# Infini-attention block on one core: stack loads moved eight slots later, maxima issued two slots sooner, and three small moves around the feed-forward part

## The chip, the core and the metric

The kernel runs on one core of a Trainium2 chip. The metric is the device time of one execution in microseconds (us); runs before and after are compared by the median of several. Five engines work side by side, each taking its own instructions in order: TensorE (PE in the profile; its weight loads PEld), VectorE (DVE), ScalarE (ACT), GpSimd (POOL) and SyncE (SP), which here only issues DMAs. ACT issues some DMAs as well.

## The reference, cut to what matters

A transformer block: adaptive layer norm, attention with a compressive memory (32 heads of 16, 4 segments of 512 rows), output projection, residual, a second layer norm, a feed-forward part of width 1792, residual.

```python
mod = (_silu(c) @ w_mod).reshape(c.shape[0], 6, 1, -1)
sa, ca, ga, sb, cb, gb = (mod[:, 0], mod[:, 1], mod[:, 2], mod[:, 3], mod[:, 4], mod[:, 5])
h = _layernorm(x, axis=-1) * (1 + ca) + sa
x = x + ga * _A_ref(h, A_wq, A_wk, A_wv, A_wo, A_beta)
h = _layernorm(x, axis=-1) * (1 + cb) + sb
x = x + gb * _B_ref(h, B_w1, B_b1, B_w2, B_b2)
...
# _A_ref, for each segment s of 512 rows (all heads):
logits = jnp.einsum("bhqd,bhkd->bhqk", qs, ks) * scale + mask
p = _softmax(logits, axis=-1)
a_dot = jnp.einsum("bhqk,bhkd->bhqd", p, vs)
num = jnp.einsum("bhld,bhde->bhle", pq, M)
den = jnp.einsum("bhld,bhd->bhl", pq, z)[..., None] + 1e-6
o = g * (num / den) + (1.0 - g) * a_dot
M = M + jnp.einsum("bhld,bhle->bhde", pk, vs)
z = z + jnp.einsum("bhld->bhd", pk)
```

x is 2048 x 512 in float32; products are formed from high and low halves, which gives three matmuls where one would do in plain precision.

## The kernel before

Up to about 180 us the conditioning, the projections and the memory parts run. From 180 to 470 us runs the attention, in loops. From 470 us the feed-forward part (FFN) runs, in products that combine sums of blocks (t1 to t4, b11 to b22).

**Stacks and loops.** The heads and segments are cut into 32 stacks Q of four heads, each with two pairs P = 2Q and 2Q + 1. A stack's keys and queries lie in two SBUF tiles, `kst` and `qst`, with four buffers each (Q modulo 4). `load_stacks(Q)` (L172 to L175) fetches rows 0 to 95 of both from DRAM with two DMAs of 384 KB on SP, kst first. One pass of the loop over Q (L1013) does, for the pairs of stack Q, the T parts (`st_part`, scores with queries along the free axis, PE L693, exp on ACT L708 and L719, causal cut on POOL L696) and the products with V (L733), and for the pairs of stack Q + 2 the S parts (`s_part`, PE L606 and L643 to L645, row maxima on DVE L613 and L617). S1 of stack Q + 2 is the first thing in loop Q: its weight loads and matmuls wait for the two loads of stack Q + 2. The order inside a loop is written out:

```python
ORDER = ('S1 c0 T2 T3 T2 c1 S2 c2 S3 T3 S3 c3 c4 c5 T5 S0 c6 c7 T0 c8 c9 '
         'T1 T4 S2 c10 c11 T5 S1 c12 T4 S0 c13 T0 c14 T1 c15 c16 c17 c18 c19')
```

S and T with a number are parts of `s_part` and `st_part`. c0 to c19 are twenty slots; a slot runs whatever has been put down for it. The table `PRM` (L27 to L75) gives places as slot numbers: a number d for stack Q means slot 20Q + d, counted from the start of loop 0, so -65 is c15 of loop Q - 4 and -57 is c3 of loop Q - 3. Each engine gets its instructions in the order in which the loop issues them.

**The maxima's way.** The row maxima of a stack (`nm`) are needed by its T parts as three further rows of `qst` (96 to 98). `m_rows` (POOL L661, two subtractions, slot -26) splits them into three bf16 parts; `m_put` (L664 to L669, slot -17) turns them with a matmul against the identity into a PSUM bank (PE L667, tile `pv`) and copies that on ACT (L127, tile `ms`, 48 x 128); `m_send` (L675) follows one slot later and writes 12 KB into the query stack by DMA, issued by SP for stacks 0 to 12 and by ACT for stacks 13 to 31 (`msa` 13). The first reader is the first T2 of loop Q. There is one `pv` bank, which the V products of each loop and `m_put` share; the copy `ts` (ACT L127) empties it at a loop's start, and its store to DRAM is `TD` on SP (L751). `dn` (L756) and `opk` (L758) bring pairs of those back in every second loop; the rows of L784, L788, L913 on SP are other small or 256 KB transfers.

**Other places.** `gate` is the slot of a 256 KB load of a gate vector on SP (L989). `ht` is the slots in which the four transposed blocks of segment 0 are made for the FFN (`ln2_turn`, PE L574, ACT L576). `r_sub` (DVE L886) forms the sums t1 to t4, `r_hi` copies the high half on ACT (L127) and `r_lo` subtracts it on DVE (L899). `rest` runs leftovers of the last stacks' attention (den L775, rb_in, mix L793, o_lo L810). `quad(n)` is the FFN's first half for quarter n in numbered steps; `bg` puts work into a step, here the transposes of segments 2 and 3.

Of the kernel before, what the change touches and what calls it, by code (L numbers as in the profile page):

```python
# [28 lines left out]
 'pv': [[31, 0, 0, 512], [36, 1, 128, 512], [37, 2, 256, 512], [38, 3, 384, 512]],  # L29
 'pvlast': [[25, 0, 0, 512], [30, 1, 128, 512], [31, 3, 384, 512], [35, 2, 256, 512]],  # L30
 'mrows': -26,
 'mput': -17,
 'stacks': -65,
 'den': 95,
 'dnl': 18,
 'rbl': 13,
# [11 lines left out]
 'wox': -25,  # L48
 'mixu': 12,
 'olou': 12,  # L50
 'ht': [502, 509, 516, 523],
 'ht1': 644,
 'ln': [{'in': [327, 367, 387, 407], 'stat': [418, 425, 437, 445], 'rstd': 449, 'on': [455, 475, 479, 495]},
        {'in': [527, 530, 547, 567], 'stat': [565, 577, 585, 597], 'rstd': 603, 'on': [624, 626, 628, 630]}],
 'wl': [26, 66, 77, 81],
 'gate': 197,
# [45 lines left out]
def block_kernel(ctx: ExitStack, tc: tile.TileContext, x, wq, wk, wv, wo, betaq, betam,  # L102
# [99 lines left out]
    with ExitStack() as pa:  # L202
# [124 lines left out]
        for ds in ((0,), (1, 2, 3)):  # L327
# [4 lines left out]
            n = slice(ds[0], ds[-1] + 1)  # L332
# [24 lines left out]
        rest = ((2, 3), (4, 5))  # L357
# [155 lines left out]
        for s in range(NSEG):  # L513
            for tok in PRM["A"][s].split():
                n = int(tok[1]) if len(tok) > 1 and tok[1].isdigit() else 0
# [64 lines left out]
    mm = psw.tile([128, 512], F32, name="mm")  # L580
# [3 lines left out]
    with ExitStack() as pb:  # L584
# [295 lines left out]
        def raw(p, n):  # L880
            return T2 if n == "t2" and p == 0 else hk(p, RAW.get(n, n))

        def r_sub(p, n, e=v):
            x, y = {"t1": ("b12", "b11"), "t2": ("b22", "t1"), "t3": ("b22", "b12"), "t4": ("b21", "t2")}[n]
            for o, i, j in zip(raw(p, n), raw(p, x), raw(p, y)):
                e.tensor_tensor(out=o, in0=i, in1=j, op=ALU.subtract)  # L886
# [6 lines left out]
        def r_hi(p, n, e=None):  # L893
            for k in range(2):
                copy(e or "a", R[n][0][k], raw(p, n)[k])
# [117 lines left out]
        for Q in range(-LEAD // 2, NP // 2 + 1):  # L1013
# [4 lines left out]
            for tok in ORDER.split():  # L1018
                n = int(tok[1:])
# [15 lines left out]
    def rest(U, *names):  # L1035
        for n in names:
            for x in [x for x in left if x[0] == n and x[1] == U]:
                left.remove(x)
                x[2]()

    with ExitStack() as pc:
# [6 lines left out]
        spare = pf.tile([128, 512], F32, name="spare")  # L1048
# [10 lines left out]
        def w_views(j, i):  # L1059
            t, lo, hi, src, o = WS[i]  # L1060
            x = (wb if src else wa)[j][:, o:o + hi - lo]
            return [z.rearrange("p a k n -> p (a k n)") for z in (wt1[t][j % 2][0][:, lo:hi], wt1[t][j % 2][1][:, lo:hi], x)]
# [5 lines left out]
        def w_lo(j, i):  # L1068
            h, l, x = w_views(j, i)
            v.tensor_tensor(out=l, in0=x, in1=h.bitcast(F32), op=ALU.subtract)  # L1070
# [24 lines left out]
        def bg(n, i, f, *a):  # L1095
            bgs.setdefault((n + i // 7, i % 7), []).append((f, a))
# [73 lines left out]
        r_lo(0, "t1")  # L1170
        r_hi(0, "t2")
        w_lo(0, 1)
        rest(15, "den", "rb_in")
        rest(14, "mem_mix")
        r_lo(0, "t2")
# [26 lines left out]
        for n in range(2 * FH):  # L1202
# [6 lines left out]
            if j + 1 < FH and n:  # L1209
                for i in range(7):  # L1210
                    bg(n, i, w_prep, n + 1, i)
        for n, i, f, *a in ((0, 0, rest, 14, "o_hi", "o_lo"), (0, 0, r_sub, 0, "t3"), (0, 0, r_sub, 0, "t4"), (0, 1, w_hi, 0, 2), (0, 1, w_hi, 0, 3),
                            (0, 3, r_hi, 0, "t3"), (0, 3, wo_late, 2, 3), (0, 3, r_lo, 0, "t3"), (0, 3, w_hi, 1, 0),
                            (0, 4, w_lo, 1, 0), (0, 4, w_lo, 0, 2), (0, 4, w_lo, 0, 3), (0, 4, load_w1, 2),
                            (0, 4, r_hi, 0, "t4"), (0, 4, rest, 15, "mix", "o_hi"), (0, 4, r_lo, 0, "t4"),
                            (0, 4, rest, 15, "o_lo"), (0, 5, g_out, 0, s1, s1, 0, 0), (0, 6, w_hi, 1, 1),
                            (2, 2, ln2_load, 2, 0), (2, 3, ln2_load, 2, 1), (2, 5, ln2_load, 2, 2), (2, 6, ln2_load, 2, 3),
                            (1, 0, w_lo, 1, 1), (1, 0, r_hi, 0, "b22"), (1, 1, wo_late, 3, 4),
                            (1, 1, w_hi, 1, 2), (1, 1, w_hi, 1, 3), (1, 1, r_lo, 0, "b22"), (1, 2, close_wo),
                            (1, 3, w_lo, 1, 2), (1, 3, w_lo, 1, 3)):  # L1220
            bg(n, i, f, *a)
# [14 lines left out]
        for s, n in ((2, 3), (3, 4)):  # L1236
            for b in range(4):
                bg(n, 1 + b, ln2_stats, s, b)
            bg(n, 5, ln2_rstd, s)
            for i in range(2):  # L1240
                bg(n, 8 + i, ln2_applies, s, 2 * i, 2 * i + 2)
            for d in range(KB):
                bg(n, 14 + d, ln2_turn, s, d, (mm, spare)[d % 2])

        w2r = {}

# [50 lines left out]
        for p in range(2):  # L1297
            n = FH * p + FH - 1
# [56 lines left out]
        for p in range(2):  # L1355
            for j in range(FH):
                quad(FH * p + j, j == 0)
            n = FH * p + FH - 1
# [3 lines left out]
            for m in range(NM):  # L1362
                s, f = 2 * p + m // FB, m % FB
# [68 lines left out]
```

## Time and profile before

| what | value |
|---|---|
| median of 3 runs | 785.66 us (785.25 to 789.05) |
| the profiled execution: time | 784.93 us |
| the profiled execution: span, first to last instruction | 783.2 us |
| PE busy | 764.9 us, 98% of the span |
| DVE, ACT, POOL busy | 555.9, 472.4, 316.3 us |
| granted TensorE clock | 1.000 |
| DMA moved | 156.09 MB, mean 199 GB/s |

The profile is of one execution, and 1.73 us lie outside its span. Rows of the timeline give the start in us, the length in us, the engine, the line, the operation with output<-input, and how many like instructions follow each other (x2); a bracket gives the idle time of the engine just before and what ended it. SPq and ACTq are DMA issues on the queues of SP and ACT. A row in the waits list is the waiting engine and line, the engine or DMA that released it, the sum of waits in us, how many, and the longest.

### The profile page before, as it was taken

To read this page: it belongs to the slowest core of one execution; us is meant where nothing else is said; L and a number is where in the kernel's file an instruction comes from. 1 tells how busy PE (TensorE), PEld (TensorE's weight loads), DVE (VectorE), ACT (ScalarE), POOL (GpSimd) and SP (SyncE) were. 2 spreads that over 40 slices of the span, in tenths; PEclk is the share of its full clock that TensorE was granted. 3 is DMA by queue.
4 is the path that set the end of the run, shared out by engine and by line. 5 is a ranking of instruction groups with operands and counts; after the bars stand their busy time and mean duration, and the time that the engine had idled before them with its cause. 6 is when DMAs were issued, how large, how long until landed. Compare 5 with 4: busy or idle time off the path is not lost.

```text
span 783.2 us, 14171 instructions
## 1 busy us (share of the span) xinstructions
PE 764.9 (98%) x4549; PEld 529.0 (68%) x4549; DVE 555.9 (71%) x1540; ACT 472.4 (60%) x910; POOL 316.3 (40%) x535
## 2 busy tenths in 40 slices
PE   9999999999999999999989999999999999999998
PEld 4877786877444445454445457787888888888887
DVE  6677677548989888888977898868569764432424
ACT  3465546364888877777768676766644446652221
POOL 1256458261468556665786671242000404200000
PEclk9999999999999999999999999999999999999999
DMA  9596956487465576768677755595666524545543
GB/s 337 185 295 228 317 179 221 166 275 258 139 187 166 175 207 190 212 205 243 185 188 210 222 156 166 184 309 177 202 240 208 184 95 162 172 148 166 173 126 116
DMA packets 108818, 156.09 MB, mean 199 GB/s; under 512 B 16324, under 2 KB 55620, under 8 KB 108744
## 3 DMA queue, kind: packets, MB, share of 16 engines
q1 hardware_dynamic: 106911, 153.39, 62.1%
q10 hardware_dynamic: 1833, 1.81, 0.7%
q8 instruction: 35, 0.57, 0.3%
q14 instruction: 39, 0.32, 0.1%
HBM read 93.95 MB, written 60.83 MB: 198 GB/s over the span
## 4 chain that ended last, share of the span: by engine, by line
PE 76%; DVE 8%; POOL 5%; DMA 4%; issue 4%; ACT 3%; ACTq 0%; SPq 0%; DVEq 0%; POOLq 0%
PE bx L1080 9%; PE att L693 6%; PE pv L733 6%; PE q L313 6%; PE bx L1349 6%; PE att L606 5%; PE by L1349 5%; PE bv L1349 5%; PE bv L1080 5%; PE k L313 4%; PE v L464 3%; PE mm L821 3%; DMA qst<-ms 3%; PE spare L1349 2%; PE by L1080 2%
## 5 line engine op out<-in xcount | busy, mean ns | idle before, releaser
L613 DVE CUSTOM_DVE_ANT_0 dump<-att,maskb 128x384 bf16<-128x384 f32 (+1 forms) x456 | 207.7, 512 | 36.2 <-PE att L606 17.9
L708 ACT ACTIVATE pt<-att 128x384 f32<-128x384 f32 (+1 forms) x256 | 125.6, 545 | 17.7 <-PE att L693 14.1
L696 POOL TENSOR_SCALAR_AFFINE_SELECT pt<-pt 128x256 f32<-128x256 f32 x256 | 105.5, 425 | 67.9 <-ACT pt L708 42.4
L693 PE MATMUL att<-qst,kst 99*128 99x256 bf16 (+3 forms) x512 | 107.7, 300 | 7.3 <-DMA qst<-ms 5.4
L606 PE MATMUL att<-kst,qst 96*128 96x384 bf16 (+1 forms) x456 | 103.9, 310 | 1.1 <-ACT pt L719 0.4
L693 PEld LDWEIGHTS <-kst 99*128 99x128 bf16 x512 | 43.8, 97 | 74.9 <-issue 37.7
L865 POOL TENSOR_TENSOR wb<-wa 128x256 f32<-128x256 f32 x24 | 20.1, 838 | 154.2 <-DMA wa<-in_w 123.1
L733 PE MATMUL pv<-pt,V 128*32 128x512 f32 (+1 forms) x992 | 79.8, 439 | 0.0
L719 ACT ACTIVATE pt<-att 128x256 f32<-128x256 f32 (+1 forms) x128 | 62.2, 494 | 27.8 <-PE att L693 15.4
L136 DVE TENSOR_TENSOR gl<-s,gh 128x512 fp32r<-128x512 f32 x34 | 24.1, 710 | 42.0 <-ACT gh L133 42.0
L606 PEld LDWEIGHTS <-qst 96*128 96x128 bf16 x456 | 37.9, 98 | 21.6 <-issue 14.2
L733 PEld LDWEIGHTS pv<-pt,V 128*32 128x32 f32 x992 | 25.8, 109 | 36.0 <-issue 30.4
L133 ACT ACTIVATE gh<-s 128x512 fp32r<-128x512 f32 x34 | 21.3, 628 | 46.8 <-PE spare L1349 18.7
L1085 ACT ACTIVATE s<-s,b1t 128x512 f32<-128x512 f32 x42 | 30.3, 722 | 21.3 <-DVE s L1089 21.1
L1089 DVE TENSOR_TENSOR s<-bv,s 128x512 f32<-128x512 f32 x28 | 19.2, 687 | 32.2 <-PE bv L1080 22.8
L613 DVE DVE_READ_ACCUMULATOR2_ANT nm<- 128x1 f32 x456 | 38.1, 84 | 0.0
L509 POOL TENSOR_TENSOR q<-qr,q 128x512 bf16<-128x512 f32 x16 | 18.7, 1167 | 27.7 <-ACT q L508 27.3
L500 POOL TENSOR_SCALAR qp<-qp 128x512 f32<-128x512 f32 x12 | 19.2, 1596 | 25.2 <-ACT qp L495 25.2
L136 DVE TENSOR_TENSOR w1ml<-s,w1mh 128x512 fp32r<-128x512 f32 x18 | 13.0, 721 | 21.6 <-ACT w1mh L133 21.6
L661 POOL TENSOR_TENSOR nm<-nm 128x16 f32<-128x16 f32 x64 | 13.9, 217 | 33.8 <-DVE nm L613 31.1
L133 ACT ACTIVATE w1mh<-s 128x512 fp32r<-128x512 f32 x18 | 11.3, 628 | 26.1 <-PE spare L1349 11.6
L313 PE MATMUL q<-Ahl,wqh 128*128 128x512 f32 x64 | 25.8, 404 | 0.2 <-DVE Ahl L136 0.2
(362 smaller groups left out, 2041.0 us busy)
## 6 DMA issues: line engine op xcount, KB each, us to landing
GD<-s SPq DMA_DIRECT2D x56, 256.0 KB
s<-GD SPq DMA_DIRECT2D x52, 256.0 KB
kst<-KD SPq DMA_DIRECT2D x32, 384.0 KB
qst<-QD SPq DMA_DIRECT2D x32, 384.0 KB
TD<-ts SPq DMA_DIRECT2D x32, 256.0 KB
xt<-X2D SPq DMA_DIRECT2D x28, 256.0 KB
wa<-in_w SPq DMA_DIRECT2D x28, 256.0 KB
QD<-q SPq DMA_DIRECT2D x16, 384.0 KB
```

The costliest lines, as they stand in the source:

```text
L133: act.activation(hi, src, AF.Copy)
L136: lo_eng.tensor_tensor(out=lo, in0=src, in1=hi.bitcast(F32), op=ALU.subtract)
L313: pe.matmul(ps, a[:, k, 128 * g:128 * g + 128], b[k], start=(k == 0 and i == 0), stop=(k == KB - 1 and i == 2))
L606: pe.matmul(ps, q_of(P, h, i), k_of(P, h, 128 * (i + 1)), start=True, stop=True)
L613: v.tensor_tensor_reduce(out=dump[n_dump[0] % 2][:, :n], in0=src, in1=maskb[:, 512 - n:], scale=-1.0, scalar=-4 * NEG, op0=ALU.add, op1=AL ...
L693: pe.matmul(ps, k[:99, e, 128 * j:128 * j + 128], q[:99, e, 128 * j:512], start=True, stop=True)
L696: pool.affine_select(out=t, in_=t, pattern=pattern, compare_op=ALU.is_ge, fill=0.0, base=0, channel_multiplier=-1)
L708: act.activation(pt[:, h, :], ps[:, :n], AF.Exp, scale=0.25)
L719: act.activation(pt, pv_, AF.Exp, scale=0.25)
L733: pe.matmul(ps[32 * c:32 * c + 32, lo:hi], V[4 * s + j][:, VW * hd:VW * hd + 32], pt[:, c % 2, lo - o:hi - o], start=start, stop=stop)
L1080: pe.matmul(ps, a[:, i, k, :], b[k], start=start and k == 0 and c == 0, stop=k == 1 and c == 2, skip_group_check=not start)
L1349: pe.matmul(ps, a[:, c], w[:, lo:hi], start=(f == 0 and i == 0), stop=(last and i == 2))
```

## The change

Six edits; no instruction is added or taken away:

```diff
- 'mput': -17,
- 'stacks': -65,
+ 'mput': -19,
+ 'stacks': -57,
...
- 'ht': [502, 509, 516, 523],
+ 'ht': [505, 512, 519, 526],
...
- 'gate': 197,
+ 'gate': 209,
...
         w_lo(0, 1)
+        r_sub(0, "t3")
         rest(15, "den", "rb_in")
...
-        for n, i, f, *a in ((0, 0, rest, 14, "o_hi", "o_lo"), (0, 0, r_sub, 0, "t3"), (0, 0, r_sub, 0, "t4"), (0, 1, w_hi, 0, 2), (0, 1, w_hi, 0, 3),
+        for n, i, f, *a in ((0, 0, rest, 14, "o_hi", "o_lo"), (0, 0, r_sub, 0, "t4"), (0, 1, w_hi, 0, 2), (0, 1, w_hi, 0, 3),
...
-                bg(n, 14 + d, ln2_turn, s, d, (mm, spare)[d % 2])
+                bg(n, (13 + 2 * d) if s == 2 else 14 + d, ln2_turn, s, d, (mm, spare)[d % 2])
```

`m_put(Q)` goes from c3 to c1 of loop Q - 1, and with it `m_send(Q)` from c4 to c2. `load_stacks(Q)` goes from c15 of loop Q - 4, right behind the last T part that reads the buffer, to c3 of loop Q - 3, one slot behind `m_send(Q - 2)`. One line is added ahead of the FFN's steps, so lines after L1173 have a number higher by one in the changed kernel.

On SP, the first four loops' rows before the change. `ms` is the maxima on their way into a query stack; of the loads, those of stacks 2, 3, 4, 5 and 6 stand here in this order:

```order
L175 DMA kst_2076<-KD_1_90 96x2048
L175 DMA qst_2075<-QD_1_74 96x2048
L675 DMA qst_1832<-ms_2169 3x16x128
L175 DMA kst_2141<-KD_1_90 96x2048
L175 DMA qst_2140<-QD_1_74 96x2048
L675 DMA qst_1837<-ms_2238 3x16x128
L175 DMA kst_1833<-KD_2_91 96x2048
L175 DMA qst_1832<-QD_2_75 96x2048
L675 DMA qst_2075<-ms_2322 3x16x128
```

The same stretch of SP's queue in the changed kernel:

```order
L675 DMA qst_1832<-ms_2142 3x16x128
L175 DMA kst_2076<-KD_1_90 96x2048
L175 DMA qst_2075<-QD_1_74 96x2048
L675 DMA qst_1837<-ms_2221 3x16x128
L175 DMA kst_2139<-KD_1_90 96x2048
L175 DMA qst_2138<-QD_1_74 96x2048
L675 DMA qst_2075<-ms_2305 3x16x128
L175 DMA kst_1833<-KD_2_91 96x2048
L175 DMA qst_1832<-QD_2_75 96x2048
```

Each load of a stack Q up to 14 now stands right behind the send of the maxima of stack Q - 2; before, it stood ahead of that send, with the send of the stack before it in front. From stack 15 on no send stands on SP, since ACT issues them, and the load stands behind the store TD.

On PE, a piece of the difference in the loop before the first T part (the matmuls of L464 make V there; `nm` is the maxima as POOL leaves them):

```order
 L606 MATMUL att_2066<-kst_1838,qst_1837 128x384
+L667 LDWEIGHTS nm_2054
+L667 MATMUL pv_2068<-identb,nm_2054 128x128
 L464 MATMUL mm<-wvh,Ahh_0_1730 128x512
 L464 MATMUL mm<-wvh,Ahl_0_1731 128x512
```

The transposing matmul of `m_put(0)`, which stood behind both S3 of that loop, now stands right behind S1's two matmuls and in front of all V matmuls of the loop. In the later loops it moves in the same way from behind the second S3 to a place ahead of S2.

On ACT, a piece of the difference in loop 0 (the exps of the first T parts, and the copy `ms`):

```order
+L708 ACTIVATE pt_1_2211<-att_2067 128x384
+L708 ACTIVATE pt_1_2211<-att_2062 128x384
+L708 ACTIVATE pt_1_2217<-att_2063 128x384
+L127 ACTIVATE ms_2221<-pv_2068 48x128
+L708 ACTIVATE pt_1_2217<-att_2066 128x384
 L719 ACTIVATE pt_3_2241<-att_2062 128x256
```

The copy was behind the fourth of these exps and is now ahead of it.

## The prediction

> **What bounds the kernel now.** I read the page first, then the busy time by stretches, then who waits for whom on TensorE (PE) and on SyncE's queue (SP). The page:
>
> ```profile
> PE 764.9 (98%) x4549; PEld 529.0 (68%) x4549; DVE 555.9 (71%) x1540; ACT 472.4 (60%) x910; POOL 316.3 (40%) x535
> ```
>
> PE is busy for 764.9 of 783.2 us. Every instruction stays in the program, so an edit can only change PE's idle time: at most 18.3 us is there to win, and any new wait of PE is a loss in full. The stretches of the attention stage and the start of the FFN (columns: length, then PE, PEld, DVE, ACT, POOL busy, clock, DMA share, GB/s) show where the idle time is:
>
> ```profile
> 230.00:270.00 40.00, 39.50 (x349) 19.29 (x350) 35.91 (x143) 35.35 (x78) 30.26 (x64) 1.00 0.58 173
> 270.00:310.00 40.00, 38.46 (x333) 19.50 (x329) 33.44 (x146) 30.81 (x69) 21.63 (x52) 1.00 0.71 200
> 390.00:430.00 40.00, 37.05 (x305) 19.39 (x305) 30.04 (x133) 30.25 (x65) 31.10 (x55) 1.00 0.71 192
> 470.00:500.00 30.00, 28.15 (x150) 21.36 (x149) 24.67 (x40) 18.63 (x32) 6.32 (x6) 1.00 0.52 163
> ```
>
> The loops of 230 to 270 have half a microsecond of idle time in 40; those of 390 to 430 have 2.95. The clock is 1.00 in all of them. The waits between 180 and 500 us (us in total, times, longest) name the cause:
>
> ```profile
> PE att L693 <- DMA qst<-ms: 5.4, 6, 2.4
> PE bx L1080 <- DVE rt3l L899: 1.2, 1, 1.2
> ```
>
> Six of the loops begin with PE waiting for the 12 KB of row maxima (`ms`) that L675 sends into the query stack; one wait at the head of the FFN is for the low half of t3. On SP the stack loads themselves wait:
>
> ```profile
> SPq L175 <- PE att L693: 65.6, 26, 5.8
> ```
>
> SP stands 65.6 us at the kst load, since it is placed right behind the last reader of the buffer. What stands behind it on SP waits with it. The change takes that wait away, and this is its plain merit.
>
> **The change, part by part.** *1. Loads behind the maxima, loops with the send on SP.* The rows of loop 5 (PE, ACT, SP) and the S1 that opens loop 6:
>
> ```profile
> 232.86 0.50 PE L606 MATMUL att<-kst,qst 96*128 96x384 bf16 x2
> 240.49 0.50 PE L606 MATMUL att<-kst,qst 96*128 96x384 bf16 x2
> ```
>
> ```profile
> 232.99 0.60 ACT L127 ACTIVATE ts<-pv 128x512 f32<-128x512 f32 x1
> 233.56 1.73 ACT L708 ACTIVATE pt<-att 128x384 f32<-128x384 f32 x4
> 235.19 0.26 ACT L127 ACTIVATE ms<-pv 48x128 bf16<-48x128 f32 x1
> ```
>
> ```profile
> 231.52 0.32 SPq L175 DMA_DIRECT2D kst<-KD  x1
> 235.47 0.78 SPq L675 DMA_DIRECT2D qst<-ms  x1
> ```
>
> A loop is 240.49 − 232.86 = 7.63 us. Before, the load is issued at 231.52, 1.34 us ahead of loop 5, and its first reader is the S1 of loop 6 at 240.49: 8.97 us for the load. After, it stands behind the send. The copy of `ms` goes one exp sooner (1.73 / 4 = 0.43 us), so the send at 235.47 becomes 235.04; with its 0.78 us SP reaches kst at about 235.85, 3.0 us into the loop. That leaves 7.63 − 3.0 = 4.6 us instead of 8.97. How long a load takes: one that has the queues to itself was issued at 201.71, one with neighbours at 231.52.
>
> ```profile
> 201.71 0.31 SPq L175 DMA_DIRECT2D kst<-KD  x1
> ```
>
> ```profile
> 201.70:202.60 0.90, 0.72 (x3) 0.29 (x3) 0.90 (x4) 0.89 (x2) 0.23 (x1) 1.00 0.00 0
> 202.60:206.10 3.50, 3.18 (x27) 1.90 (x29) 3.50 (x15) 2.98 (x8) 2.01 (x6) 1.00 0.74 225
> 206.10:207.00 0.90, 0.90 (x9) 0.06 (x3) 0.90 (x5) 0.87 (x2) 0.41 (x1) 1.00 0.22 41
> 236.00:236.60 0.60, 0.60 (x9) 0.35 (x10) 0.60 (x3) 0.60 (x2) 0.60 (x3) 1.00 0.66 235
> 236.60:237.20 0.60, 0.60 (x8) 0.00 (x0) 0.60 (x3) 0.60 (x2) 0.60 (x2) 1.00 0.27 72
> ```
>
> Nothing moves for 0.9 us; then 3.5 us at 225 GB/s are 787 KB, which is the pair of 384 KB stacks. So the bytes are there 4.4 us after issue. The load of 231.52 still ran at 235 GB/s until 236.6: 5.1 us, with other transfers beside it. From the last byte to the instruction that it releases no row shows the time alone: between nothing and the 0.9 us that the start took; I take the half, 0.45. So a load is usable 4.85 us after issue alone, and 5.55 with neighbours; the ends are 4.4 and 6.0. Against the 4.6 that are left, PE waits 0.25 or 0.95 us per loop (ends: nothing, and 1.4). The neighbours, dn and opk of the attention output, come in every second loop, so the mean is 0.6. The stacks 4 to 14 are loaded so, in eleven loops: **+6.6 us** (0 to 15). In these loops PE has only half a microsecond of idle time in 40 that could absorb any of it. The eight slots later alone would cost nothing (the load would be issued at the loop's start); what costs is that on SP, which is in order, it has to stand behind a send which waits for ACT's copy.
>
> *2. The start.* In the loop before the first T part, S1, POOL's subtraction and the next events are:
>
> ```profile
> 187.90 0.50 PE L606 MATMUL att<-kst,qst 96*128 96x384 bf16 x2
> 188.98 0.51 POOL L661 TENSOR_TENSOR nm<-nm 128x16 f32<-128x16 f32 x2 [5.56 <-DVE nm L613]
> 188.72 1.90 ACT L170 ACTIVATE kst<-one 32x2048 bf16<-32x2048 f32 x1
> 195.94 0.50 PE L606 MATMUL att<-kst,qst 96*128 96x384 bf16 x2
> 198.57 0.78 SPq L675 DMA_DIRECT2D qst<-ms  x1
> 201.75 0.48 PE L606 MATMUL att<-kst,qst 96*128 96x384 bf16 x2
> ```
>
> The multiplication L667 that turns the maxima now stands right behind S1, whose last matmul gives way at 188.10, but POOL is ready at 188.98 + 0.51 = 189.49; behind L667 twelve matmuls of V stand on PE and wait too. That is **+1.4**. ACT then copies after its 1.90 us fill (190.62), SP sends and loads stack 2 from about 191.7, usable at 196.6 to 197.3; its S1 at 195.94 has moved to 197.3 by the 1.4, so nothing more. In loop 0 the send of 198.57 becomes 198.1, the load of stack 3 starts at 198.9 and is usable at 203.8, against an S1 at 201.75 (both later by 1.4): **+2.0** (1.6 to 3.1).
>
> *3. The waits for the maxima.* Two of the six, and what is late beside the longest:
>
> ```profile
> 280.30 0.50 PE L693 MATMUL att<-qst,kst 99*128 99x384 bf16 x2 [1.02 <-DMA qst<-ms]
> 404.47 0.66 PE L693 MATMUL att<-qst,kst 99*128 99x384 bf16 x3 [2.42 <-DMA qst<-ms]
> 403.93 0.51 POOL L661 TENSOR_TENSOR nm<-nm 128x16 f32<-128x16 f32 x2
> ```
>
> In loop 11 the send leaves SP ahead of the load of its loop: **−1.0**. The five others (5.4 − 1.0 = 4.4) lie in loops where L675 is issued by ACT. There SP no longer stands in front of a send, and the loads start right after the store TD, some 1 to 2 us into the loop. Loop 14 as it is now, with the send in the chain of waits and the S1 behind it:
>
> ```profile
> 308.08 6.95 DMA qst<-ms
> ```
>
> ```profile
> 306.55 0.67 SPq L751 DMA_DIRECT2D TD<-ts  x1
> ```
>
> ```profile
> 313.72 0.50 PE L606 MATMUL att<-kst,qst 96*128 96x384 bf16 x2
> ```
>
> The 12 KB took 6.95 us behind other transfers. After, the send comes 0.4 us sooner, the load at 307.22 instead of early in the loop before; usable at 312.1 to 312.8, against an S1 at 313.72: no wait, with 0.9 to 1.6 us to spare. The 12 KB land behind it, ahead of the T part that needs them at 314.2. So these waits go, but of the 2.42 only half counts: POOL's subtraction for the next stack ends at 403.93 + 0.51 = 404.44, and L667 stands behind it and now 2 slots sooner. **−3.2** (−4.4 to 0).
>
> The Trainium skill, "DMA: Bandwidth & Descriptors", section "Queues, rings and completion order", says that a DMA engine takes turns between the queues that have work, packet by packet; by this an ACT-issued send would pass beside SP's loads, and the sum would be 1.2 lower (rival D). The trace does not agree: the 12 KB of 308.08 took 6.95 us on a queue of their own.
>
> *4. L667 in front of POOL later on.*
>
> ```profile
> 433.46 0.38 PE L606 MATMUL att<-kst,qst 96*128 96x256 bf16 x2
> 434.79 0.51 POOL L661 TENSOR_TENSOR nm<-nm 128x16 f32<-128x16 f32 x2
> ```
>
> In loop 28 the new place of L667 is ahead of 433.46, and POOL ends at 435.30: 1.84 us, with S2, T3 and the wo matmuls of the loop behind it. About 0.8 of it PE waits today at later points of the loop: **+1.0** (0 to 1.8). In other loops POOL is ready ahead of the place.
>
> *5. The FFN's head and the transposes.*
>
> ```profile
> 480.14 0.35 DVE L775 RECIPROCAL dn<-dn 128x32 f32<-128x32 f32 x1 [1.27 <-DMA dn<-TD]
> 484.68 2.39 DVE L886 TENSOR_TENSOR hr<-hr,hr 128x512 f32<-128x512 f32 x2
> 539.23 0.66 PE L574 MATMUL mm<-ident,xt 128*128 128x128 f32 x4 [0.71 <-ACT hr L576]
> ```
>
> The two subtractions of t3 (2.39 us where they stand) move into DVE's idle 1.27 us ahead of 480.14. Everything behind them, rt3l among it, comes sooner by the shorter of that and PE's wait of 1.2: **−1.0** (1.2 less some delay of dn). Transposes two steps apart rather than one give ACT the time to empty the bank: **−0.7**. The moves of segment 0's transposes by three slots and of the gate vector's 256 KB load by twelve change which loop carries them; loops 25 and 10 hide them in the same way as their neighbours: 0 (−0.5 to 1).
>
> Sum: 6.6 + 1.4 + 2.0 − 1.0 − 3.2 + 1.0 − 1.7 = **+5.1 us**. The profiled execution took 784.93 us (span 783.2), so it would take 790.0. The median of the runs is 785.66, 0.7 above it; I put the change on the median: **790.8 us**.
>
> **Rivals.**
> *A. The load is in time (not slower).* If a load is usable at most 4.5 us after issue in the loops of the first half, no S1 waits, and terms 1 and the 2.0 of the start vanish: 790.8 − 8.6 = 782.2. For it: the bytes need 4.4 us, and the neighbours of 231.52 may be issued after the load once it stands later. Against it: the release after the last byte, and a margin of 0.2 us that every neighbour eats. It decides at 4.6 us.
> *B. The late half gains nothing.* The load goes out 0.4 us ahead of the send there, with opk, am and TD queued ahead of both. If transfers run at the pace of the 6.95 us, kst is usable about at the next S1, and the send still waits: 3.2 not gained, and some 0.3 us in each of 14 loops: 790.8 + 7.4 = 798.2. It also says that the change does not do what its words say for stacks from 15 on, since there the load is not held behind the send by any queue.
> *C. POOL decides.* If L667 waits for POOL in loops 23, 24 and 28 in full (margins of about −1.2, −0.5 and −1.8, of which 0.8 is counted as absorbed): +2.5, 793.3.
> *D. ACT's sends overtake.* If the 12 KB that ACT issues pass beside SP's transfers once no other send is in front, all of the 4.4 goes instead of 3.2: 789.6. The 6.95 us row speaks against it.
>
> **How the numbers follow.** The forecast has 0.43 (its own range 787.5 to 794.5, by the 0 to 0.95 per loop), A 0.22, B 0.15, C 0.12, D 0.04, anything else 0.04. The range reaches from A with its late half in full (781.0) to B (798.0). A measurement of this kernel tells about 0.5%, 3.9 us, from no change: 781.7 and 789.6. Faster: less than half of A and some of the rest, 0.13. Within: the rest of A and a third of the forecast, 0.31. Slower: 0.56.
>
> **What would show it.** The SP wait of L175 on L693 disappears. S1 (L606) at the loop starts from 201 to 300 us shows idle time put down to DMA kst or qst, and the loops there are 7.9 to 8.6 us instead of 7.63. L667 waits for POOL near 189 and 436. The waits for `ms` at L693 go from six to at most one or two. rt3l's 1.2 and the 0.71 of the transposes are gone. I am wrong if the first-half loops stay at 7.63 (A), or if L693 still waits for `ms` after 300 us (B).

## The result and the profile after

The changed kernel took **794.94 us** (median of 4 runs, 793.45 to 797.3), the kernel before 785.45 us in the same runs (median of 4): a ratio of 1.0102, with a 95% interval of 1.0071 to 1.0134. Run once more beside two of the experiments it gave 1.0123 (1.0098 to 1.0147). So it is slower by 8 to 10 us; 790.8 had been forecast, with 781.0 to 798.0 as the range.

The page of the changed kernel, and the waits of PE between 180 and 510 us (us in total, times, longest):

```profile
PE 766.5 (97%) x4549; PEld 529.4 (67%) x4549; DVE 556.8 (70%) x1540; ACT 471.0 (59%) x910; POOL 315.6 (40%) x535
```

```profile
PE att L606 <- DMA qst<-QD: 12.4, 13, 2.5
PE pv L667 <- POOL nm L661: 2.4, 3, 1.1
...
PE att L693 <- DMA qst<-ms: 0.2, 1, 0.2
```

And two rows of SP's waits in the same stretch:

```profile
SPq L784 <- DVE dn L776: 69.0, 14, 7.0
...
SPq L175 <- PE att L693: 3.7, 13, 0.4
```

The waits for the maxima at L693 fell from 5.4 us to 0.2. In their place stand 12.4 us at L606: S1 waits for the two loads of its stack, thirteen times. SP waits 3.7 us at L175 instead of 65.6, but it still stands: 69.0 us at L784, a small store, where it stood 17.3 us before. L667, the multiplication that now comes sooner, waits 2.4 us for POOL.

To see what each stretch of the program is worth, both spans are cut at the same instructions: S1 of loop -1, S1 of loop 2, S1 of loop 13, and the first T2 of loop 31. First before, then after (columns: length, then busy time of PE, PEld, DVE, ACT, POOL, clock, DMA share, GB/s):

```profile
187.90:210.01 22.11, 21.16 (x147) 12.43 (x146) 20.48 (x82) 15.41 (x31) 7.53 (x22) 1.00 0.36 105
210.01:296.62 86.61, 84.29 (x745) 41.34 (x742) 75.20 (x302) 73.52 (x162) 57.06 (x125) 1.00 0.63 183
296.62:462.12 165.50, 159.77 (x1301) 81.88 (x1297) 140.99 (x601) 123.80 (x269) 111.23 (x215) 1.00 0.72 207
462.12:783.20 321.08, 315.28 (x1490) 256.77 (x1490) 191.83 (x309) 160.14 (x279) 51.88 (x65) 1.00 0.54 175
```

```profile
187.38:214.27 26.89, 22.69 (x146) 13.04 (x146) 20.99 (x82) 15.48 (x31) 7.46 (x22) 0.94 0.38 99
214.27:308.97 94.70, 85.04 (x745) 41.41 (x742) 75.21 (x302) 72.72 (x162) 56.81 (x125) 1.00 0.59 168
308.97:472.14 163.17, 159.74 (x1301) 82.17 (x1297) 139.77 (x600) 123.15 (x268) 108.85 (x213) 1.00 0.73 211
472.14:791.70 319.56, 315.19 (x1490) 256.95 (x1490) 193.57 (x311) 160.22 (x279) 53.63 (x67) 1.00 0.54 176
```

The start of the loops costs 4.8 us, loops 2 to 12 cost 8.1, loops 13 to 30 give 2.3 back and the rest 1.5. The changed execution comes to the first cut 0.5 us sooner; less this, the sum is the 8.5 us between the spans (783.2 and 791.7).

How a loop pays is seen in loop 4 of the changed kernel, behind which S1 waits longest of all loops from 2 on. PE's S1 that opens it and the one that opens loop 5; ACT's copy; SP's queue; and the DMA in the stretches between:

```profile
231.57 0.50 PE L606 MATMUL att<-kst,qst 96*128 96x384 bf16 x2 [1.17 <-DMA qst<-QD]
```

```profile
240.69 0.50 PE L606 MATMUL att<-kst,qst 96*128 96x384 bf16 x2 [1.44 <-DMA qst<-QD]
```

```profile
232.27 1.25 ACT L708 ACTIVATE pt<-att 128x384 f32<-128x384 f32 x3 [1.19 <-PE att L693]
233.40 0.26 ACT L127 ACTIVATE ms<-pv 48x128 bf16<-48x128 f32 x1
```

```profile
233.68 0.79 SPq L675 DMA_DIRECT2D qst<-ms  x1
234.57 0.38 SPq L175 DMA_DIRECT2D kst<-KD  x1
235.01 0.40 SPq L175 DMA_DIRECT2D qst<-QD  x1
235.51 0.37 SPq L913 DMA_DIRECT2D wor<-in_wo  x1
```

```profile
234.57:235.50 0.93, 0.93 (x9) 0.45 (x11) 0.93 (x3) 0.86 (x2) 0.93 (x3) 1.00 0.06 13
235.50:238.00 2.50, 2.50 (x22) 0.96 (x18) 2.23 (x11) 1.99 (x5) 2.50 (x6) 1.00 0.91 224
238.00:240.10 2.10, 1.25 (x24) 0.52 (x16) 1.38 (x6) 1.90 (x4) 1.05 (x4) 1.00 0.83 212
```

The copy of `ms` comes behind three exps, the send at 2.11 us into the loop, kst at 3.00. For 0.93 us no byte of the stack moves (the 12 KB of the send do), then 4.6 us at 212 to 224 GB/s are about 1.0 MB: the 786 KB of the stacks and most of the 256 KB wor load, which stands right behind the stacks on the queue in loops 1 to 4 and shares the transfer. The packet records put the stack's last byte at 240.10, and S1 starts 0.59 us later. Nine of the loops from 3 to 12 begin late by this chain, by 0.95 us on the mean, and since ACT's copy waits for the loop's own first T parts, the lateness is passed on to the next load.

### The profile page after: what moved, and what is told of

Its sections match the earlier page's. It is cut to its first block, busy times and chain, and to the rows that moved or that the text cites. A ratio compares the mean times of both kernels' runs of the same rounds, so it can differ in the third digit from the quotient of the medians.

```text
span 791.7 us, 14187 instructions
## 1 busy us (share of the span) xinstructions
PE 766.5 (97%) x4549; PEld 529.4 (67%) x4549; DVE 556.8 (70%) x1540; ACT 471.0 (59%) x910; POOL 315.6 (40%) x535
## 4 chain that ended last, share of the span: by engine, by line
PE 75%; DMA 11%; DVE 5%; issue 3%; ACT 3%; POOL 2%; SPq 0%; DVEq 0%; ACTq 0%
PE bx L1080 9%; DMA qst<-QD 7%; PE att L693 6%; PE q L313 6%; PE att L606 5%; PE bx L1350 5%; PE by L1350 5%; PE bv L1350 5%; PE bv L1080 5%; PE pv L733 5%; PE k L313 4%; PE mm L821 3%; PE v L464 3%; PE spare L1350 2%; PE by L1080 2%
## 5 line engine op out<-in xcount | busy, mean ns | idle before, releaser
L606 PE MATMUL att<-kst,qst 96*128 96x384 bf16 (+1 forms) x456 | 104.8, 311 | 13.3 <-DMA qst<-QD 12.4
L693 PE MATMUL att<-qst,kst 99*128 99x256 bf16 (+3 forms) x512 | 108.2, 302 | 1.1 <-DMA qst<-ms 0.2
L693 PEld LDWEIGHTS <-kst 99*128 99x128 bf16 x512 | 45.1, 98 | 68.8 <-issue 38.7
L719 ACT ACTIVATE pt<-att 128x256 f32<-128x256 f32 (+1 forms) x128 | 62.5, 493 | 13.9 <-PE att L693 13.6
L606 PEld LDWEIGHTS <-qst 96*128 96x128 bf16 x456 | 36.9, 98 | 32.3 <-DMA qst<-QD 17.7
L509 POOL TENSOR_TENSOR q<-qr,q 128x512 bf16<-128x512 f32 x16 | 18.7, 1166 | 27.3 <-ACT q L508 26.9
L313 PE MATMUL q<-Ahh,wqh 128*128 128x512 f32 x64 | 26.0, 407 | 0.0
```

Source lines behind the costliest of these rows:

```text
L313: pe.matmul(ps, a[:, k, 128 * g:128 * g + 128], b[k], start=(k == 0 and i == 0), stop=(k == KB - 1 and i == 2))
L606: pe.matmul(ps, q_of(P, h, i), k_of(P, h, 128 * (i + 1)), start=True, stop=True)
L693: pe.matmul(ps, k[:99, e, 128 * j:128 * j + 128], q[:99, e, 128 * j:512], start=True, stop=True)
L719: act.activation(pt, pv_, AF.Exp, scale=0.25)
```

## Experiments

All ratios are to the kernel before on the same chip, with 95% intervals, from five rounds each. The four stretches are cut in each kernel's trace as above; the last column is what follows the first T2 of loop 31.

| kernel | ratio | loops -1 to 1 | loops 2 to 12 | loops 13 to 30 | rest |
|---|---|---|---|---|---|
| before | 1 | 22.1 | 86.6 | 165.5 | 321.1 |
| the change | 1.0102 (1.0071 to 1.0134) | 26.9 | 94.7 | 163.2 | 319.6 |
| the change again | 1.0123 (1.0098 to 1.0147) | 28.4 | 95.8 | 163.1 | 321.3 |
| load ahead of send | 1.0016 (0.9996 to 1.0035) | 24.1 | 87.4 | 168.8 | 318.4 |
| load's place alone | 1.0019 (0.9994 to 1.0045) | 22.1 | 86.1 | 166.7 | 322.7 |
| maxima alone | 1.0027 (1.0003 to 1.0052) | 24.1 | 86.5 | 165.4 | 322.3 |
| FFN edits alone | 0.9982 (0.9956 to 1.0008) | 22.1 | 86.8 | 166.6 | 319.8 |
| early half as before | 0.9943 (0.9923 to 0.9962) | 22.1 | 86.2 | 163.7 | 320.1 |
| start as before | 1.0063 (1.0039 to 1.0086) | 23.5 | 95.3 | 163.3 | 320.2 |
| sends on ACT | 1.0051 (1.0030 to 1.0073) | 24.4 | 92.4 | 165.7 | 322.2 |
| load first, 24 and 29 late | 0.9934 (0.9905 to 0.9963) | 22.1 | 86.3 | 165.6 | 320.9 |
| load first, plain | 0.9941 (0.9920 to 0.9962) | 22.1 | 86.6 | 163.1 | 319.2 |
| half the bytes | 0.9979 (0.9956 to 1.0001) | 28.2 | 85.5 | 164.2 | 319.9 |

**The load ahead of the send.**

```diff
- 'stacks': -57,
+ 'stacks': -59,
```

> The changed kernel with the load two slots sooner (-59), so that on SP it stands ahead of the store TD and of the send instead of behind the send. Theory (what costs is the place behind a send that waits for ACT's copy; six of the eight slots alone cost nothing): the load is issued near the start of the loop, the 12 waits of S1 for the loads between 201 and 301 us (11.2 us) go, the waits for the maxima stay away, the 1.1 of the first multiplication and the gains late and in the feed-forward part stay: 785.45 + 1.4 - 1.0 - 2.3 - 1.5 = 782.0 us. Rival 1 (loads are too late because they run beside other transfers, wherever they stand on SP): S1 still waits 0.5 or more per loop, 788 to 792. Rival 2 (the send now lies behind the load's bytes): S1 does not wait, but T2 waits for the maxima again in the first half, 0.5 per loop, 787.

Measured: 1.0016. The first half behaved as the theory has it: loops 2 to 12 take 87.4 us instead of 94.7, and the waits of S1 between 180 and 310 us are 1.5 us in two:

```profile
PE att L606 <- DMA qst<-QD: 1.5, 2, 1.1
```

With neither TD nor the send of its loop in front of it on SP, the load goes out 1.3 us ahead of the loop (216.78 against an S1 at 218.12), as in the kernel before, and the loss is gone, so rival 1 falls there. Whether the place or the time does it, the next run tells. The time as a whole missed the 782.0, since the late half, which had given 2.3 us, lost 3.3: S1 waits 4.1 us there, 2.5 of it at stack 31, whose load was issued behind five other DMAs.

```profile
434.12 0.60 SPq L756 DMA_DIRECT2D dn<-TD  x1
434.77 0.57 SPq L758 DMA_DIRECT2D opk<-TD  x1
435.38 0.46 SPq L765 DMA_DIRECT2D amB<-AMD  x1
435.88 0.60 SPq L770 DMA_DIRECT2D rm<-rdd  x1
436.52 0.46 SPq L830 DMA_DIRECT2D xb<-in_x  x1
437.09 0.62 SPq L175 DMA_DIRECT2D kst<-KD  x1
```

The first of them waited 2.9 us for the store TD. A place ahead of the send is also a place behind whatever stands in that slot.

**The load's place alone.**

```diff
- 'stacks': -65,
+ 'stacks': -57,
```

(edited in the kernel before)

> The kernel before with the loads' place alone moved (-57); the multiplication and the send stay at -17 and -16, so the load stands behind TD and ahead of the send. Theory (the send in front is the cost): S1 does not wait, 785.45 less what the load no longer holds up on SP (1.0 of loop 11 and about half of the 4.4 of the later loops): 782 to 784. Rival 1 (eight slots later are too late by themselves): S1 waits 0.5 to 1 per loop in the first half, 791 to 796. Rival 2 (the send lies behind the load's bytes): T2 waits for the maxima in most loops, 0.3 each, 793.

Measured: 1.0019. In the first half eight slots later are not too late by themselves: with the send still behind the load, kst goes out 1.2 us into the loop instead of 3.0, loops -1 to 1 are unchanged at 22.1 us and loops 2 to 12 are 0.5 shorter, since loop 11's wait of 1.02 is gone and one of 0.39 is new. The late half did not gain its two microseconds; it lost 1.2 (S1 waits 3.2 us in four, T2 1.6 in four).

**The maxima alone.**

```diff
- 'mput': -17,
+ 'mput': -19,
```

(edited in the kernel before)

> The kernel before with the multiplication and the send alone two slots sooner (-19), loads at -65. Theory (sooner maxima alone move a send by 0.4 us, and cost where L667 stands in front of POOL): 1.4 at the start, at most 0.4 off each of six waits for the maxima, 0.7 + 0.5 of waits of L667 late: 785.45 + 1.4 - 2.0 + 1.2 = 786.0, 1.001 of before. Rival (the late gain of the change came from the sooner maxima, not from the loads): 785.45 + 1.4 - 1.0 - 2.3 = 783.5, 0.9976.

Measured: 1.0027. The rival falls: the late half stays at 165.4. L667 waits for POOL 3.4 us in three, 1.1 of it at the start and 1.6 in loop 28; the start costs 2.0. So neither move alone gave the late gain: the loads alone +1.2 there, the maxima alone -0.1, both together -2.3. Both together are not always enough: the kernel with all sends on ACT, below, has both moves there and ends at 165.7.

**The FFN edits alone.**

```diff
- 'mput': -19,
- 'stacks': -57,
- 'ht': [505, 512, 519, 526],
- 'gate': 209,
+ 'mput': -17,
+ 'stacks': -65,
+ 'ht': [502, 509, 516, 523],
+ 'gate': 197,
```

(edited in the changed kernel, which leaves the move of t3's subtractions and the spreading of segment 2's transposes)

> The kernel before with the feed-forward edits alone (the subtractions of t3 at the head, segment 2's transposes two steps apart). Theory: both PE waits go (1.2 for the low half of t3, 0.7 for the transposes), 1.5 less, as the two profiles differ behind the last loop: 783.9. Rival (the gain there came only because the attention ended later against the same DMAs): rt3l still waits, at most 0.7 less, 784.7.

Measured: 0.9982, 1.4 us less, but with an interval that touches no change. The trace agrees in size: 319.8 us behind the loops instead of 321.1, and rt3l waits 0.3 instead of 1.2. The moves of segment 0's transposes and of the gate vector's load are undone here too; no run has them alone.

**The early half as before.**

```diff
-            ap(20 * Q + PRM["stacks"], load_stacks, Q)
+            ap(20 * Q + (PRM["stacks"] if Q > 14 else -65), load_stacks, Q)
...
-            ap(20 * Q + PRM["mput"], own, "pv", ("m", Q), m_put, (Q,), True)
-            ap(20 * Q + PRM["mput"] + PRM["msl"], m_send, Q)
+            mp = PRM["mput"] if Q > 12 else -17
+            ap(20 * Q + mp, own, "pv", ("m", Q), m_put, (Q,), True)
+            ap(20 * Q + mp + PRM["msl"], m_send, Q)
```

> The changed kernel with stacks up to 14 loaded at -65 and the multiplications and sends of stacks up to 12 at -17, as before; everything from stack 15 on, and the feed-forward edits, as in the change. Theory (all of the loss is in loops -1 to 13, where SP issues the sends): PE waits as before until 300 us, then the gains: 785.45 - 2.3 - 1.5 = 781.6. Rival (part of the loss is a lower clock or DMA contention over the whole attention): 785 or more.

Measured: 0.9943 (781.85 us), by the ratio 4.5 us below before. All of the loss lies where SP issues the sends; the rival falls.

**The start as before.**

```diff
-            ap(20 * Q + PRM["stacks"], load_stacks, Q)
+            ap(20 * Q + (PRM["stacks"] if Q > 3 else -65), load_stacks, Q)
...
+            mp = PRM["mput"] if Q > 1 else -17
```

(with `mp` used as in the kernel above)

> The changed kernel with the start undone: stacks 2 and 3 loaded at -65 and the multiplications and sends of stacks 0 and 1 at -17; the rest as in the change. Theory (the start costs the 1.1 at the first multiplication, the 2.5 of stack 3's S1 and, behind that wait, 1.1 of lowered clock in loop 1): loops -1 to 1 take 22.1 us as before instead of 26.9, the clock in loop 1 reads 1.00, and the time is 4.8 less than the changed kernel's 1.0102 of before: 1.004 of before. Rival (the wait only moves on: stack 4's S1 takes it over): at most 2 less, 1.0075 of before, with a new wait of about 2 at the S1 that opens loop 2.

Measured: 1.0063, 3 us below the changed kernel, between the two. Loops -1 to 1 take 23.5 us, with clock 1.00 in loop 1; but the first S1 behind a late load, now stack 4's, takes a wait over:

```profile
209.90 0.50 PE L606 MATMUL att<-kst,qst 96*128 96x384 bf16 x2 [0.97 <-DMA qst<-QD]
```

**All sends on ACT.**

```diff
- 'msa': 13,
+ 'msa': 0,
```

> The changed kernel with all sends of the maxima issued by ACT (msa 0 instead of 13): the loads stay in their slot, but no send stands in front of them on SP. Theory (what costs is SP standing at the send): S1 does not wait in loops 0 to 12, the gains late and in the feed-forward part stay, the 1.1 at the first multiplication stays: 785.45 + 1.4 - 1.0 - 2.3 - 1.5 = 782.0, that is 0.996 of before, plus 0.73 us of issue on ACT per loop where ACT has no slack. Rival 1 (the slot itself is too late): S1 still waits 0.5 to 1 in each loop, 1.008 to 1.012. Rival 2 (ACT's sends lie behind the loads' bytes): T2 waits for the maxima in the first half, 0.3 to 0.5 per loop, 1.001 to 1.003.

Measured: 1.0051, outside both the theory's number and the rivals'. In the first half S1's waits for loads fall from 11.1 us to 0.9, as the theory has it, but each loop has a new wait of PE, where the theory had only added ACT's issue time in case ACT had no slack:

```profile
PE att L693 <- ACT pt L708: 4.7, 11, 0.5
```

```profile
230.52 0.27 ACT L127 ACTIVATE ms<-pv 48x128 bf16<-48x128 f32 x1
230.82 0.76 ACTq L675 DMA_DIRECT2D qst<-ms  x1
231.62 0.49 ACT L708 ACTIVATE pt<-att 128x384 f32<-128x384 f32 x1 [0.83 <-PE att L606]
```

The issue holds ACT for 0.76 us, to 231.58, between the third and the fourth exp (the matmul that the last row names was done at 231.36); the fourth exp empties its bank 0.8 us later, and the next T part that needs the bank waits 0.36 to 0.50 us. A loop like this one takes 8.25 us, where 7.62 were needed before the change: moving the send off SP takes S1's wait of 0.95 away and leaves the loop 0.6 longer than it was, by this new wait for the most part.

**Half the bytes.** For stacks 4 to 14 only rows 0 to 47 are loaded, so the scores of these stacks are computed from stale rows in part.

```diff
-            sp.dma_start(st[:96], dd[s][g].rearrange("c r e n -> (c r) e n")[:, 4 * t:4 * t + 4, :])
+            n = 48 if 4 <= Q <= 14 else 96
+            sp.dma_start(st[:n], dd[s][g].rearrange("c r e n -> (c r) e n")[:n, 4 * t:4 * t + 4, :])
```

> The changed kernel with 48 instead of 96 rows loaded for each of stacks 4 to 14 (half the bytes, so scores of these stacks come from stale rows; nothing else changes). Theory (S1 waits since a load that is issued 3.0 us into a loop of 7.6 needs 5.0 for its bytes and 0.6 to release): half the bytes take 2.5 less, the ten waits from 222 to 301 us (8.8 us) go altogether, stack 3's 2.5 at the start stays: 1.0102 less 0.011 = 0.999 of before. Rival (a fixed place, not the bytes: the loads wait for something else on the queues): the waits stay above 0.5 each, 1.006 or more.

Measured: 0.9979, against 1.0123 for the changed kernel in the same runs. Every wait of S1 for a load between 206 and 310 us is gone, and loops 2 to 12 take 85.5 us. The stack's last byte comes 3.5 us behind the issue instead of 5.0 (mean of stacks 5 to 14), 1.5 us sooner, where 2.5 had been expected. That is as much as the longest of the waits, 1.44, so the same place is early enough, and the fixed-place rival falls.

**The change once more**, beside the last three.

> The changed kernel once more, beside the other two on one chip: 1.0102 of before (1.007 to 1.013), S1's waits for the loads at 11 to 13 us in sum, and a lowered clock in loop 1 behind the wait of about 2.5.

Measured: 1.0123; S1 waits 13.0 us in twelve; loop 1 as below, in the part on the hardware.

**Two versions with the load first.** In both, the multiplication stays at -17 while SP sends, so that the load passes in front of the send; the first keeps stacks 24 and 29 at -17 as well.

```diff
+            mp = -17 if Q < 13 or Q in (24, 29) else PRM["mput"]
```

> A version that should beat both: the changed kernel with the multiplications at -17 for stacks 0 to 12 (so the load stands ahead of the send on SP) and for stacks 24 and 29 (where L667 waited for POOL). Theory: no loss in the first half, loop 11's 1.0 gained, the late gains with 1.2 less waiting for POOL, feed-forward gain: 785.45 - 1.0 + 0.4 - 2.3 - 1.2 - 1.5 = 779.9, 0.993 of before. Rival (waits only change places: in the late half every load or send that is in time makes another late): as the kernel with the early half of before, 0.994 to 0.996.

Measured: 0.9934, which fits the theory's number and, by its interval, the rival's; the stretches decide for the rival. Where L667 waited no longer for POOL in loop 23, T2 waited 0.85 for the maxima and S1 of stack 27 then 2.07 for its load, and the late half ended at 165.6, as before the change.

```diff
+            mp = -17 if Q < 13 else PRM["mput"]
```

> The changed kernel with the multiplications at -17 for stacks 0 to 12 only, so that the load stands ahead of the send on SP while SP sends, and all later stacks as in the change (stacks 24 and 29 too). Theory: the first half loses nothing, loop 11's wait goes, loops 23 to 25 are as in the changed kernel (9.4, 9.3, 10.3 us) instead of 8.6, 11.7 and 11.6: 0.992 to 0.994 of before. Rival (the late half comes out differently in each kernel, by which transfers meet): 0.995 to 1.000, with a wait of 1 or more at an S1 or T2 after 300 us.

Measured: 0.9941 (0.9920 to 0.9962), 782.9 us. Its profile has the start and the first half of before, the late half and the rest of the change (163.1 and 319.2), as its theory says. This is a version that beats both kernels, by 0.6% and 1.8%; the three versions between 0.9934 and 0.9943 can't be told apart by their intervals.

## Why the prediction was right, and where its size was not

- **What bounds the kernel** held: PE's busy time hardly moved (764.9 to 766.5), and the time follows PE's waits. (One slip ahead of the prediction: the rows of SP's queue shown with the change are the loads of stacks 2 to 4, not 2 to 6.)
- **Loads behind the maxima**, forecast +6.6 less loop 11's 1.0, measured +8.1 for loops 2 to 12. The mechanism was shown from four sides: the load ahead of the send two slots sooner and in the same slot, the send taken off SP, the bytes halved. The size was off in the time a load needs. kst is issued 2.99 us into the loop on the mean of stacks 4 to 14 (3.0 forecast); the stack's last byte comes 4.93 us behind that (4.75 as the mean of 4.4 alone and 5.1 with neighbours); S1 starts 0.63 us after it, where half of 0.9, 0.45, had been taken. That makes 0.9 us per loop instead of 0.6.
- **What a load needs**, in that sum. The 5.1 was a misreading that came out near by luck: in the packet records the load of 231.52 had its last byte at 236.06, 4.54 us after issue, and what ran on until 236.6 was the store TD. Nor did the neighbours split the loops into two kinds. Of the changed kernel's loads the five with dn and opk behind them needed 4.99 us on the mean (4.65 to 5.31), the other six 4.89; among these, the three with only a 256 KB wor load behind them took 4.57 to 5.53, the one with the gate vector's 5.26, and the two with nothing behind them on SP 4.39 and 4.94. What spreads them is not shown. In all nine S1s waited 0.95 us on the mean, instead of eleven 0.6; stack 9's waited 0.2, and stack 4's not at all, behind the slow loop 1.
- **The start**, forecast +3.4, measured +4.8. The first multiplication waited 1.14 us and its loop grew by 1.4, as forecast; stack 3's S1 waited 2.48 (2.0). Left out was what follows such a wait: loop 1 ran at a lowered clock and took 1.1 us more of PE time.

```profile
189.02 0.23 PE L667 MATMUL pv<-identb,nm 128*128 128x128 bf16 x1 [1.14 <-POOL nm L661]
```

- **The waits for the maxima late and L667 behind POOL**, forecast -3.2 and +1.0, measured -2.3 together. L667 waited 0.53 at 444.6, which is loop 28 as forecast, but half of the 1.0; and 0.70 at 398.0 in loop 23, where the forecast had POOL ready and only rival C had a wait. Only half of the 2.42 was gained, as forecast, but not for the reason given: no L667 waited in its loop 25; the 0.70 in loop 23 and 0.66 of S1 waiting for the load of stack 27 took the other half. In the experiments neither move alone gave any of the late gain.
- **The FFN**, forecast -1.7, measured -1.5 (in the second profile of the changed kernel the stretch took 321.3 us, so the size is not sure to a microsecond). Neither rt3l's nor the transposes' wait is left; the slow pair on DVE only changed its owner. In the changed kernel the pair of t3 takes 1.28 us, and that of t4 the 2.39:

```profile
489.37 1.28 DVE L886 TENSOR_TENSOR hr<-hr,hr 128x512 f32<-128x512 f32 x2
...
495.30 2.39 DVE L886 TENSOR_TENSOR hr<-hr,s 128x512 f32<-128x512 f32 x2
```

- **Rival A** (the load in time) fell by the 12.4 us at L606; **B** (the late half gains nothing) fell for the change as it is, though six experiments landed there, 165.4 to 168.8, three of them with both moves in the late half; **C** named loop 23 rightly but fell by its size, since POOL's waits there and in loop 28 come to 1.2. **D** can't be told from the forecast by a total: of 5.4 us of waits for the maxima 0.2 are left, but the 12 KB did not overtake: in the packet records they took 4.3 to 8.4 us on ACT's queue, against 1.7 to 7.7 before. What they gained is the start: ACT issues them at least 6.8 us ahead of the first T2 in every late loop but the last, where it was 6.0 before.

What stays open: which transfers must meet for one long wait in the late half (stack 31 in one kernel, stack 27 in another). Each variant moved it, and no run isolates a single transfer there. The stretches are from one profile of each kernel, so differences of a microsecond in the late half and the rest are not sure.

## What to carry to other kernels

On an in-order DMA queue a transfer's place is set by what stands in front of it, and by what that waits for: in the first half eight slots alone cost nothing, and with the send in front as well nine loops began 0.95 us late. Ahead of such a move, add up issue, bytes with their new neighbours, and the release of the waiting engine, and compare the sum with the time to the first reader; here 2.99 + 4.93 + 0.63 = 8.55 stood against 7.63. And a wait that is taken from one queue shows up on the next in-order engine: look at what the issue itself holds up there.

## What the runs showed of the hardware

I had not expected a lowered granted clock behind a PE wait of about two microseconds. In the trace's clock records it is 1.00 or 0.50, and each lowered stretch within these kernels lasts 3.41 or 6.83 us; the rows below average over it. Stretches behind the wait of 2.48 us in the changed kernel (PEclk is the third number from the end):

```profile
205.33:208.00 2.67, 2.67 (x14) 1.74 (x15) 1.65 (x7) 1.39 (x4) 0.41 (x1) 0.58 0.00 0
208.00:211.00 3.00, 3.00 (x22) 1.33 (x19) 2.82 (x11) 2.21 (x5) 1.00 (x3) 0.80 0.48 127
211.00:214.27 3.27, 3.27 (x38) 1.49 (x35) 2.46 (x10) 2.30 (x5) 1.66 (x5) 1.00 0.81 209
```

And behind the 2.60 us in its second profile:

```profile
204.65:207.65 3.00, 3.00 (x14) 1.80 (x15) 1.60 (x7) 1.39 (x4) 0.41 (x1) 0.50 0.00 0
207.65:210.65 3.00, 3.00 (x14) 1.49 (x12) 2.30 (x8) 1.86 (x5) 0.82 (x2) 0.50 0.47 111
```

PE is busy all the time there and does the work of loop 1 in 8.94 and 10.31 us, where 8.25 were needed with 0.44 us of waits among them. The same followed waits of 1.95, 2.07, 2.21 and 2.50 us in four experiments; the wait of 2.42 us in the kernel before was followed by 1.00. So of seven waits over 1.9 us six were followed by it, and one was not. Shorter ones were, too: one of 1.36 us that ended at 284.16 in the changed kernel's second profile, and one of 1.45 us behind the loops with all sends on ACT.

```profile
284.16:287.16 3.00, 2.92 (x19) 1.78 (x20) 2.54 (x11) 2.09 (x6) 0.88 (x3) 0.82 0.59 207
287.16:290.20 3.04, 3.04 (x15) 0.96 (x13) 1.92 (x8) 1.57 (x3) 2.35 (x4) 0.61 0.54 129
```

Waits of 1.84, 1.69 and 1.60 us in three other experiments were followed by 1.00. So the length of the wait does not decide it alone, and no run isolates what does. The Trainium skill, "TensorE: Matmul & The Clock Gate", section "Part 1: The HAM clock gate (the "warmup" mystery)", names about 3.4 us of idle time as what brings the clock down; here the clock came down with no wait longer than 2.60 us before it, so the measurement decides. In the FFN-edits-alone kernel it fell on the wait in loop 25, which took 15.9 us instead of 13.6, although no edit touches that loop.
